# One change to an attention and two-expert-stage kernel: the second product's first operands are made a step earlier, its weights loaded tile by tile, and the start's hand-set order is written anew

## The chip, the cores and the metric

The kernel runs on one core of a Trainium2 chip. The metric is device time of one execution in microseconds (us); the lower the better. The engines named here are PE (TensorE, matrix products), DVE (VectorE, elementwise), ACT (ScalarE, activations and copies), POOL (GpSimd) and SP (SyncE, which issues nearly all DMAs). PEld is PE's weight load, which overlaps its matmuls.

## The reference, cut to what matters

```python
kv = np.einsum('bhsd,bhse->bhde', k, v)          # 4 batches, 8 heads, 576 rows, 64 columns
out = np.einsum('bhsd,bhde->bhse', q, kv)
x = out / np.sqrt(np.mean(out * out, axis=-1, keepdims=True) + 1e-06) * g_norm
x = x.transpose(0, 2, 1, 3).reshape(2304, 512)
x = ((x @ w_a) * (x @ w_b)) @ w_out              # w_a, w_b 512 x 1536, w_out 1536 x 512
h = x @ w_in                                     # w_in 512 x 2048
g = np.maximum(h, 0.0) + np.log1p(np.exp(-np.abs(h)))
return (g @ w2_out).astype(np.float32)           # w2_out 2048 x 512
```

All inputs are float32 or (the weights) 64-bit floats that the kernel itself narrows.

## The kernel before, in words

**Numbers in two halves.** Almost every matrix product is done three times, on a high and a low half of each operand (`P3`: high x high, high x low, low x high). Making the halves is called a split: ACT copies the value into the high half (L166, `half_hi`), then DVE subtracts that from the value and writes the low half (L169, `half_lo`). A split of a 128x512 tile is thus one ACT and one DVE instruction. In the traces `w` is a split weight, `x` a split attention output, `op` a split operand of the last two products, `ghl` a split gate.

**First part, the script.** Attention runs by batch (0 to 3) and head pair (0 to 3), the gated stage by slots: a slot is one block of 512 (or 256) rows with one of 12 chunks of 128 columns, and makes `a` and `b` (L951 in the first 12 slots, L922 after) out of weights `raw` that DMAs bring, DVE and ACT narrow (L190, L194, L199) and a split halves. The first 12 slots and all of the attention are written out by hand, word by word, in the string `SCRIPT`; with manual scheduling, PE, DVE, ACT and POOL run their instructions in that order. A word is a number (weight item, slot or batch), a letter and sometimes a further number: `W` load a weight (L182), `A`, `B`, `c` narrow it, `d` its high half, `e` its low half on DVE, `f` its low half on POOL; `k` and `K` load keys and values (L234, L235, L229, tile `kvraw`), `Q` queries (L288), `M` multiplies keys and values (L255), `O` queries by that product; `a0` to `b3` are the quarters of a slot. `H12` with no number ahead are 12 matmuls on constants (L964) that compute nothing and only keep PE at work.

**Middle.** The rest of the gated stage, slots 12 to 59, and its second product (L424).

**Last part, two pairs of row blocks.** The softplus stage does blocks 1 and 2 together (pair 0), then blocks 3 and 4 (pair 1), by a scheme that saves one product in eight: seven products in place of eight, each from sums and differences of the four quarters. For each pair, `stage1` is run for eight column pairs i; a step makes seven products (`x`, `y`, `z`, `v`, L591), adds them on DVE (L602) and takes softplus (`soft`: DVE L579, ACT L582, DVE L584), which gives four tiles `g` per step. `g_sums` (POOL, L654 and L655) makes the sums that the second product needs; it is called for step i - 1 in step i, and for the last step after it. In pair 1 a step also does the small block 0 (`single1`, `single2`: L792, L769, L775, tiles `h`, `gs`, `ghl`, `out`).

After the eight steps of a pair comes `stage2_2`: seven turns (`TURNS`: A11, S2, A12, S3, S1, A22, S4) of eight steps, 56 steps of 12 matmuls 128x256 (L750). A step needs one split operand `op` (ACT L166, DVE L169) and one half tile of weights `w2o`, loaded by DMA (L669). `operand` also issues one POOL subtraction for each operand of A11 (L690) and of A12 (L692), in place, after the split has read the tile. Operands are made three steps ahead (`AHEAD`). Weights are loaded a whole turn at a time, at the turn's first step for the next turn: four tiles, eight DMAs. `leave` takes a finished sum out of PSUM at a turn's end (L704 on DVE, L709 on ACT) and some of them are stored. In pair 0 this stage also carries, at the steps listed in `OPS_AT`, the 14 pieces of `op_steps(1)`, which make the split operands of pair 1's first stage out of `y` (L169 `op<-y`, L480, L481, L482, L499).

From slot 12 on, instructions of an engine go in the order that the scheduler gives them, which follows the program's order and its dependences. An engine works strictly in its order: an instruction that waits holds all behind it. SP's queue follows the program's order throughout.

Where `phase2` goes from one stage to the other, before:

```python
while flow:
    advance()
g_sums(i)
if pair:
    yield from single2(i)
yield from stage2_2(pair, [] if pair else list(zip(OPS_AT, op_steps(1))))
```

Of the kernel before, what the change touches and what calls it, by code (L numbers as in the profile page):

```python
# [73 lines left out]
0i 10W 1q1 1a1 0j 6f 1b1 1l1 2K 1M2 1a2 1q2 1b2 1l2 2K0 1a3 1M3 1g 2Q0 1q3 1b3 1V 2K1 1l3 2a0 1h 7B
2a1 1U 1i 2a2 2Q1 7A 8B 1O0 1j 2K2 1O1 7c 1S0 2a3 8A 9B 9A 1C0 2b0 2Q2 8c 2g 2b1 9c 1t0 2K3 10A 1O2
1S1 1u0 2b2 7d 1C1 2Q3 2b3 7f 1t1 1N0 2h 1S2 2Q 0s0 11W 1u1 1L0 1O3 2i 0s1 1E0 2j 0Q 1C2 0s2 1Q 1R0
3K 1N1 1t2 1X0 0s3 1L1 1u2 3a0 1S3 1Y0 1E1 3a1 3K0 1C3 1Z0 3a2 1R1 1N2 1H0 3Q0 1X1 3a3 1L2 1D0 2M0
1t3 3K1 1Y1 3g 2M1 1u3 1E2 1Z1 8d 3Q1 1N3 1R2 2M2 8e 3K2 1H1 1X2 3b0 1L3 1D1 9d 2M3 1Y2 1E3 3Q2 3b1
9e 2q0 3K3 3b2 1R3 1Z2 2q1 3b3 2l0 1H2 1X3 1s0 1q4 3Q3 3h 1s1 10B 1D2 3Q 3i 0O4 1Y3 2q2 1s2 0S4 3j
1s3 2q3 1Z3 0N4 0C4 2l1 4a0 1H3 1l4 0L4 4a1 1D3 11B 4a2 2l2 0E4 4a3 10c 3q0 0R4 2l3 4b0 4g 11A 4b1  # L80
0X4 10d 4b2 3q1 11c 1O4 2q4 10e 4b3 2V 0Y4 2s0 1S4 4h 2s1 11d 2U 4i 2s2 0Z4 1C4 2O0 4j 1t4 2O1 11e
0H4 2S0 2O2 1u4 2S1 0D4 2s3 2C0 3l0 5a0 2t0 3l1 5a1 2C1 2u0 2t1 5a2 2l4 2S2 2N0 3q3 2u1 5a3 2L0 3l3
5b0 5g 5b1 2E0 2C2 5b2 2t2 2N1 2R0 2u2 5b3 2L1 2X0 3s0 3q2 5h 1N4 2E1 3s1 2Y0 1L4 2N2 3l2 5i 3s2 2R1
# [1004 lines left out]
```

## Time and profile before

| | us |
|---|---|
| median of 3 runs | 882.71 (881.82 to 883.62) |
| the profiled execution, its own time | 884.52 |
| its span in the trace | 882.7 |
| busy in the span: PE | 861.1 (98%) |
| DVE | 607.0 (69%) |
| ACT | 399.4 (45%) |
| POOL | 116.8 (13%) |

The span is the stretch between the first and the last recorded instruction; the profiled execution took 1.8 us more than that. Busy time is the time in which an engine had an instruction in work. Of PE a share of 98% says that it hardly ever stood still, not that it ran at its peak: its matmuls overlap, and a matmul that runs at half clock is busy too.

### The profile page before, as it was taken

What the parts mean: (1) busy time and instruction counts of PE and PEld (TensorE: products, weight loads), DVE (VectorE), ACT (ScalarE), POOL (GpSimd) and SP (SyncE); (2) the same over time, 40 slices, a digit from 0 to 9 for tenths busy, and PEclk for the clock granted to TensorE, in tenths of its full rate; (3) what the DMA queues carried; (4) which work ended last, traced back from release to release, by engine and by line L of the source; (5) the groups of instructions that cost most, each with busy time, mean ns of one, the idle gap of its engine ahead of it and who ended that gap; (6) DMA issues with size and microseconds to landing.
All of it is one profiled execution on the core that took longest, in us unless ns stands there. A gap on an engine that the chain in (4) does not pass through costs nothing.

```text
span 882.7 us, 13219 instructions
## 1 busy us (share of the span) xinstructions
PE 861.1 (98%) x4974; PEld 745.0 (84%) x4974; DVE 607.0 (69%) x1003; ACT 399.4 (45%) x718; POOL 116.8 (13%) x80
## 2 busy tenths in 40 slices
...
GB/s 277 268 269 118 49 1 1 102 200 316 311 225 181 144 167 216 320 258 136 167 72 128 275 170 151 78 222 122 193 166 344 394 144 143 143 61 292 246 142 48
DMA packets 73070, 160.24 MB, mean 182 GB/s; under 512 B 6448, under 2 KB 41776, under 8 KB 73008
## 3 DMA queue, kind: packets, MB, share of 16 engines
...
q8 instruction: 39, 0.64, 0.3%
...
q10 hardware_dynamic: 144, 0.00, 0.0%
...
## 4 chain that ended last, share of the span: by engine, by line
PE 87%; DMA 6%; DVE 4%; SPq 1%; ACT 1%; issue 1%; DVEq 0%; ACTq 0%
PE acc L424 16%; PE acc L750 15%; PE b L922 12%; PE a L922 12%; PE x L591 5%; PE z L591 5%; PE v L591 5%; PE b L951 3%; PE a L951 3%; DMA kvraw<-in_kv 3%; PE y L591 2%; PE h L792 2%; PE acc L769 2%; DVE op L169 2%; PE o L314 1%; DMA w2o<-kept 1%
## 5 line engine op out<-in xcount | busy, mean ns | idle before, releaser
L750 PE MATMUL acc<-w2o,op 128*128 128x256 f32 x1344 | 166.2, 286 | 7.6 <-DVE op L169 4.3
L750 PEld LDWEIGHTS acc<-w2o,op 128*128 128x128 f32 x1344 | 163.9, 194 | 10.2 <-DVE op L169 6.4
L424 PE MATMUL acc<-ghl,w 128*128 128x512 f32 (+1 forms) x720 | 160.1, 369 | 0.0
L922 PE MATMUL b<-x,w 128*128 128x512 f32 (+1 forms) x576 | 146.6, 363 | 0.3 <-ACT w L166 0.3
L922 PE MATMUL a<-x,w 128*128 128x512 f32 (+1 forms) x576 | 146.6, 363 | 0.0
L424 PEld LDWEIGHTS acc<-ghl,w 128*128 128x128 f32 x720 | 125.7, 189 | 22.8 <-DVE y L454 0.2
L922 PEld LDWEIGHTS b<-x,w 128*128 128x128 f32 x576 | 101.7, 189 | 17.6 <-ACT w L166 0.7
L922 PEld LDWEIGHTS a<-x,w 128*128 128x128 f32 x576 | 102.0, 189 | 17.1
L393 DVE TENSOR_TENSOR g<-b,g 128x512 f32<-128x512 f32 (+1 forms) x60 | 38.2, 636 | 102.2 <-PE b L922 71.6
L654 POOL TENSOR_TENSOR s<-g 128x512 f32<-128x512 f32 x14 | 19.6, 1398 | 582.6 <-PE x L591 469.8
L389 ACT ACTIVATE g<-a 128x512 f32<-128x512 f32 (+1 forms) x60 | 33.2, 553 | 133.4 <-PE a L922 125.7
L169 DVE TENSOR_TENSOR op<-g,op 128x512 fp32r<-128x512 f32 x96 | 87.8, 978 | 0.1
L582 ACT ACTIVATE g<-g 128x512 f32<-128x512 f32 x64 | 39.6, 630 | 101.4 <-DVE g L579 101.2
L166 ACT ACTIVATE w<-raw 128x512 fp32r<-128x512 f32 x100 | 64.8, 670 | 17.0 <-DVE raw L199 12.3
L166 ACT ACTIVATE op<-g 128x512 fp32r<-128x512 f32 x96 | 54.0, 620 | 25.1 <-PE acc L750 16.9
L169 DVE TENSOR_TENSOR w<-raw,w 128x512 fp32r<-128x512 f32 x92 | 61.1, 686 | 3.3 <-ACT w L166 3.0
L194 ACT ACTIVATE raw<-raw 128x512 f32<-128x512 f32 x68 | 46.3, 683 | 26.7 <-DMA raw<-in_w_out 17.8
L169 DVE TENSOR_TENSOR ghl<-g,ghl 128x512 fp32r<-128x512 f32 (+1 forms) x60 | 39.2, 654 | 18.8 <-ACT ghl L166 18.7
L199 DVE SCALAR_TENSOR_TENSOR raw<-raw 128x512 int32<-128x512 int32 x68 | 49.0, 728 | 3.8 <-ACT raw L194 2.3
L166 ACT ACTIVATE ghl<-g 128x512 fp32r<-128x512 f32 (+1 forms) x60 | 35.2, 587 | 35.9 <-DVE g L393 33.6
L591 PE MATMUL v<-op,w 128*128 128x512 f32 x192 | 48.9, 389 | 0.0
L591 PE MATMUL z<-op,w 128*128 128x512 f32 x192 | 48.7, 389 | 0.0
...
## 6 DMA issues: line engine op xcount, KB each, us to landing
...
w2o<-kept SPq DMA_DIRECT2D x112, 256.0 KB, 5.0
...
```

What stands on the lines that cost most here:

```text
L166: nc.scalar.activation(out=hi, in_=src, func=AF.Copy)
L169: engine.tensor_tensor(out=lo, in0=src, in1=hi, op=ALU.subtract)
L194: nc.scalar.activation(out=high_f, in_=high_f, func=AF.Prelu, scale=HIGH_SCALE, alpha=SIGN_SCALE)
L199: nc.vector.scalar_tensor_tensor(out=low, in0=high, scalar=3, in1=low, op0=ALU.logical_shift_left, op1=ALU.bitwise_or)
L389: nc.scalar.activation(out=t, in_=a, func=AF.Copy)
L393: nc.vector.tensor_tensor(out=t, in0=b, in1=t, op=ALU.mult)
L424: nc.tensor.matmul(out=acc[j][i2][:, :n], lhsT=w[:, a, c2], rhs=g[:, c, :n], start=(opens and i == 0), stop=(closes and i == 2),)
L582: nc.scalar.activation(out=to, in_=to, func=AF.Softplus)
L591: nc.tensor.matmul(out=o, lhsT=w[:, a, (2 * k + kk) * P:(2 * k + kk + 1) * P], rhs=x[:, c, :], start=(start and kk == 0 and i == 0), stop= ...
L750: nc.tensor.matmul(out=set_[where][b][:, k * 256:(k + 1) * 256], lhsT=x[:, c, i2 * P:(i2 + 1) * P], rhs=w[:, a, :], start=(opens and cp == ...
L922: nc.tensor.matmul(out=o[:, :n], lhsT=w[:, a, kk * P:(kk + 1) * P], rhs=xhl[j, kk][:, c, :n], start=(kk == 0 and k == 0), stop=(kk == NK - ...
L951: nc.tensor.matmul(out=live[x, i], lhsT=wt[x, f][:, a, kk * P:(kk + 1) * P], rhs=xhl[j, kk][:, c, :], start=(kk == 0 and k == 0), stop=(kk ...
```

## The change

It has three parts.

**The script.** The order of the first 12 slots is written anew. All eight `f` (low half of a weight on POOL) become `e` (on DVE). Batch 0's keys and values of head pairs 1 to 3 come in one pair of DMAs in place of three. One of the 31 matmuls on constants goes. Weight 5 is loaded before batch 1's keys and values, and batch 1's head pair 3 of keys and values before the last query tile rather than after it. On PE batch 1's L255 products stand later among the slots' quarters.

**The second product.** A generator of `stage2_2` is made in the last step of `stage1` and run up to its new first `yield`: the first weight tile is loaded and the first three operands are made there, with their three L690. The rest follows where it stood. Weights are loaded one tile (two DMAs) at a time, a turn ahead.

**The pieces beside it.** `OPS_AT` moves most of the 14 pieces of `op_steps(1)` to later steps.

```diff
-OPS_AT = [4, 7, 10, 13, 18, 21, 26, 29, 34, 37, 48, 50, 52, 54]
+OPS_AT = [9, 13, 17, 21, 25, 29, 33, 36, 39, 42, 47, 49, 51, 53]
...
-H12 0k0 0K0 0Q0 0k1 0K1 0K2 0Q1 0k2 0Q2 0k3 0K3 0Q3 H4 0M0 0W 0v0 0O0 1W 0S0 0M1 2W 0N0 0v1 3W 0L0
+H12 0k0 0K0 0Q0 0k1 0K1 0Q1 0K2 0Q2 0K3 0Q3 H1 0M0 0W 0v0 0O0 1W 0S0 H2 0N0 2W 0M1 0L0 0E0 0V1 3W
...
-        def load(n):
+        def load(n, cp):
             if n < len(TURNS):
-                weights[n] = [t_load(TURNS[n][1], TURNS[n][2], (cp, cp + 1)) for cp in range(0, NCP, 2)]
+                weights[n, cp] = t_load(TURNS[n][1], TURNS[n][2], (cp, cp + 1))
...
-        load(0)
+        load(0, 0)
         for x in steps[:AHEAD]:
             operand(*x)
+        yield
+        for cp in range(2, NCP, 2):
+            load(0, cp)
...
-            if cp == 0:
-                load(n + 1)
-                if opens:
-                    set_[where] = [bank("acc") for _ in range(2)]
+            if cp == 0 and opens:
+                set_[where] = [bank("acc") for _ in range(2)]
...
-            if cp == NCP - 1:
-                weights.pop(n)
+            if cp % 2:
+                weights.pop((n, cp - 1))
+                load(n + 1, cp - 1)
...
+                    if k == 2 and i % NCP == NCP - 1:
+                        second = stage2_2(pair, [] if pair else list(zip(OPS_AT, op_steps(1))))
+                        next(second)
                     yield
...
-            yield from stage2_2(pair, [] if pair else list(zip(OPS_AT, op_steps(1))))
+            yield from second
...
-        "k": lambda b, p: kv_first(b, slice(p, p + 1)),
+        "k": lambda b, p: kv_first(b, slice(1, NK) if p else slice(0, 1)),
```

**What moves on PE in the script.** Of PE's order, the stretch in which batch 1's keys are multiplied by its values (`kvps`, two entries for each head pair); `a` and `b` are quarters of slots 1 and 2. Before, and then with the change, where head pairs 2 and 3 stand:

```order
L255 MATMUL kvps_344<-kvraw_214 64x64 x2
L255 MATMUL kvps_344<-kvraw_292 64x64 x8
L951 MATMUL a_386<-x_304,w_324 128x512 x3
L951 MATMUL b_395<-x_304,w_356 128x512 x3
L951 MATMUL a_386<-x_342,w_324 128x512 x3
L255 MATMUL kvps_344<-kvraw_214 64x64 x2
L255 MATMUL kvps_344<-kvraw_322 64x64 x8
L951 MATMUL b_395<-x_342,w_356 128x512 x3
```

```order
L255 MATMUL kvps_365<-kvraw_239 64x64 x2
L255 MATMUL kvps_365<-kvraw_301 64x64 x8
L957 MATMUL a_358<-x_331,w_337 128x512 x3
L957 MATMUL b_382<-x_331,w_348 128x512 x3
L957 MATMUL a_456<-x_208,w_363 128x512 x3
L255 MATMUL kvps_365<-kvraw_239 64x64 x2
L255 MATMUL kvps_365<-kvraw_329 64x64 x8
```

Before, head pair 3 (`kvraw_322`) stands ahead of the last quarter of slot 1's `b`; with the change (`kvraw_329`) that quarter and the first quarter of slot 2's `a` stand ahead of it.

**What moves on DVE and POOL at the end of pair 0's first stage.** First DVE; `p`, `c`, `z`, `v`, `x` belong to steps i = 6 (`_7`) and 7 (`_8`), `op_1` to `op_3` are the first three operands. Before:

```order
L602 TENSOR_TENSOR p_8_5210<-v_5207,p_8_5210 128x512
L584 SCALAR_TENSOR_TENSOR g_16_5209<-c_5262,g_16_5209 128x512
L579 TENSOR_SCALAR g_15_5208<-p_8_5210 128x512
L584 SCALAR_TENSOR_TENSOR g_15_5208<-p_8_5210,g_15_5208 128x512
L169 TENSOR_TENSOR op_1_5292<-g_1_4631,op_1_5292 128x512
L169 TENSOR_TENSOR op_2_5296<-g_3_4744,op_2_5296 128x512
L169 TENSOR_TENSOR op_3_5300<-g_5_4824,op_3_5300 128x512
```

With the change:

```order
L579 TENSOR_SCALAR g_13_5131<-x_5127 128x512
L584 SCALAR_TENSOR_TENSOR g_14_5132<-c_5158,g_14_5132 128x512
L169 TENSOR_TENSOR op_1_5235<-g_1_4626,op_1_5235 128x512
L584 SCALAR_TENSOR_TENSOR g_13_5131<-x_5127,g_13_5131 128x512
L602 TENSOR_TENSOR c_5185<-z_5129,p_7_5133 128x512
L169 TENSOR_TENSOR op_2_5239<-g_3_4739,op_2_5239 128x512
L579 TENSOR_SCALAR g_14_5132<-c_5185 128x512
L602 TENSOR_TENSOR p_7_5133<-v_5130,p_7_5133 128x512
L169 TENSOR_TENSOR op_3_5243<-g_5_4819,op_3_5243 128x512
L584 SCALAR_TENSOR_TENSOR g_14_5132<-c_5185,g_14_5132 128x512
L579 TENSOR_SCALAR g_13_5131<-p_7_5133 128x512
L602 TENSOR_TENSOR p_8_5205<-y_5200,p_8_5205 128x512
```

Before, the splits stand behind the last L584 of the first stage; with the change three of them stand among the additions and softplus pieces of step 6, ahead of all of step 7's (`p_8`). On POOL in the same place, `s_7` and `s_8` being sums of steps 6 and 7; the rows of the difference, before and then with the change:

```order
L655 TENSOR_TENSOR g_12_5065<-g_11_5064,g_12_5065 128x512
L654 TENSOR_TENSOR s_7_5226<-g_14_5137 128x512
L655 TENSOR_TENSOR g_14_5137<-g_13_5136,g_14_5137 128x512
L654 TENSOR_TENSOR s_8_5277<-g_16_5209 128x512
L655 TENSOR_TENSOR g_16_5209<-g_15_5208,g_16_5209 128x512
L690 TENSOR_TENSOR g_1_4631<-s_1_4762,g_1_4631 128x512
L690 TENSOR_TENSOR g_3_4744<-s_2_4842,g_3_4744 128x512
```

```order
L655 TENSOR_TENSOR g_12_5060<-g_11_5059,g_12_5060 128x512
L690 TENSOR_TENSOR g_1_4626<-s_1_4757,g_1_4626 128x512
L690 TENSOR_TENSOR g_3_4739<-s_2_4837,g_3_4739 128x512
L690 TENSOR_TENSOR g_5_4819<-s_3_4917,g_5_4819 128x512
L654 TENSOR_TENSOR s_7_5221<-g_14_5132 128x512
L655 TENSOR_TENSOR g_14_5132<-g_13_5131,g_14_5132 128x512
L654 TENSOR_TENSOR s_8_5287<-g_16_5204 128x512
L655 TENSOR_TENSOR g_16_5204<-g_15_5203,g_16_5204 128x512
```

Three L690 now stand ahead of the sums of steps 6 and 7; the other five follow them. In pair 1 the same move puts the three splits behind `ghl` of step 14, among the first L602 of step 15.

**What moves on DVE ahead of the 22nd operand.** Pair 0's `stage2_2`; `op_5628` and its like are splits of `y`. Before:

```order
L169 TENSOR_TENSOR op_18_5572<-g_3_4744,op_18_5572 128x512
L169 TENSOR_TENSOR op_19_5588<-g_5_4824,op_19_5588 128x512
L704 TENSOR_TENSOR s_1_5598<-acc_5465,c_1_5440 128x512
L704 TENSOR_TENSOR s_2_5606<-acc_5466,c_2_5448 128x512
L169 TENSOR_TENSOR op_20_5620<-g_7_4904,op_20_5620 128x512
L169 TENSOR_TENSOR op_21_5636<-g_9_4984,op_21_5636 128x512
L169 TENSOR_TENSOR op_22_5652<-g_11_5064,op_22_5652 128x512
L169 TENSOR_TENSOR op_5668<-y_1977,op_5668 128x512
```

With the change:

```order
L169 TENSOR_TENSOR op_21_5605<-g_9_4979,op_21_5605 128x512
L704 TENSOR_TENSOR s_1_5576<-acc_5442,c_1_5429 128x512
L704 TENSOR_TENSOR s_2_5584<-acc_5443,c_2_5437 128x512
L480 TENSOR_TENSOR s_5624<-y_1972,y_1976 128x512
L480 TENSOR_TENSOR s_5700<-y_1974,y_1978 128x512
L481 TENSOR_TENSOR y_1972<-y_1704,y_1972 128x512
L481 TENSOR_TENSOR y_1974<-y_1706,y_1974 128x512
L482 TENSOR_TENSOR y_1704<-s_5624,y_1704 128x512
L482 TENSOR_TENSOR y_1706<-s_5700,y_1706 128x512
L169 TENSOR_TENSOR op_5628<-y_1704,op_5628 128x512
L169 TENSOR_TENSOR op_22_5631<-g_11_5059,op_22_5631 128x512
```

Before, the six L480 to L482 stood between operands 11 and 15; with the change all six stand behind the two L704, directly ahead of operand 22. Up to operand 26 four splits of `y` stand there in place of six.

## Rows read from the trace of the kernel before

**Rows 1.** Windows: us; busy us (count) of PE, PEld, DVE, ACT, POOL; clock; DMA; GB/s.

```profile
20.00:46.00 26.00, 21.41 (x163) 15.65 (x163) 22.62 (x32) 18.36 (x33) 11.54 (x7) 1.00 1.05 286
46.00:212.00 166.00, 166.00 (x940) 139.27 (x940) 107.28 (x195) 111.65 (x215) 1.32 (x1) 1.00 0.38 118
212.00:400.00 188.00, 187.72 (x906) 158.28 (x906) 136.11 (x259) 90.79 (x158) 0.00 (x0) 1.00 0.62 232
400.00:577.00 177.00, 177.00 (x850) 149.35 (x849) 114.79 (x198) 56.75 (x99) 20.12 (x14) 1.00 0.43 151
628.00:673.00 45.00, 44.98 (x374) 44.83 (x374) 29.22 (x49) 18.96 (x34) 0.00 (x0) 1.00 0.61 207
```

**Rows 2.** Waits of PE: in total, times, longest.

```profile
PE acc L750 <- DVE op L169: 4.3, 4, 1.4
```

**Rows 3.** Timeline of PE, 20 to 46 us: start, length, work, idle ahead of it.

```profile
43.71 0.69 PE L255 MATMUL kvps<-kvraw 112*64 112x64 f32 x16 [1.28 <-DMA kvraw<-in_kv]
```

**Rows 4.** DMA issues, 16 to 46 us: KB each, median us to landing.

```profile
qr<-in_q SPq DMA_DIRECT2D x5, 256.0 KB, 12.0
```

**Rows 5.** The weight tiles w on POOL: ns lowest, median, highest; idle before.

```profile
L169 POOL TENSOR_TENSOR w<-raw,w x8: 1307/1613/2035, 21.9 to 52.0; 128x512 fp32r<-128x512 f32 x8
...
  ACT w L166: 25.7, 5
```

**Rows 6.** The same tiles on DVE, first 220 us.

```profile
L169 DVE TENSOR_TENSOR w<-raw,w x22: 680/684/693, 62.7 to 216.7; 128x512 fp32r<-128x512 f32 x22
...
  ACT w L166: 1.9, 3
```

**Rows 7.** Timeline of PE around the end of pair 0's first stage.

```profile
581.12 1.52 PE L591 MATMUL v<-op,w 128*128 128x512 f32 x6
585.90 0.80 PE L750 MATMUL acc<-w2o,op 128*128 128x256 f32 x2 [3.26 <-ACT op L166]
...
602.26 20.41 PE L750 MATMUL acc<-w2o,op 128*128 128x256 f32 x168 [0.90 <-DVE op L169]
```

**Rows 8.** Windows, columns as in the first group.

```profile
590.00:592.00 2.00, 2.00 (x12) 2.00 (x12) 2.00 (x3) 1.04 (x3) 2.00 (x2) 0.54 0.02 1
```

**Rows 9.** Timeline of DVE in the same part.

```profile
575.85 1.00 DVE L584 SCALAR_TENSOR_TENSOR g<-p,g 128x512 f32<-128x512 f32 x1 [0.70 <-ACT g L582]
...
578.60 0.69 DVE L602 TENSOR_TENSOR c<-v,c 128x512 f32<-128x512 f32 x1 [0.35 <-PE v L591]
...
584.25 0.42 DVE L579 TENSOR_SCALAR g<-p 128x512 int32<-128x512 int32 x1
...
586.26 12.54 DVE L169 TENSOR_TENSOR op<-g,op 128x512 fp32r<-128x512 f32 x8
...
605.74 1.88 DVE L169 TENSOR_TENSOR op<-g,op 128x512 fp32r<-128x512 f32 x3
...
614.80 1.28 DVE L704 TENSOR_TENSOR s<-acc,c 128x512 f32<-128x512 f32 x2
...
627.39 3.09 DVE L169 TENSOR_TENSOR op<-g,op 128x512 fp32r<-128x512 f32 x5
```

**Rows 10.** Timeline of POOL in the same part.

```profile
588.10 13.56 POOL L690 TENSOR_TENSOR g<-s,g 128x512 f32<-128x512 f32 x8 [0.63 <-DVE op L169]
...
614.42 8.50 POOL L692 TENSOR_TENSOR g<-g 128x512 f32<-128x512 f32 x5 [0.70 <-DVE op L169]
```

**Rows 11.** Timeline of PE around the end of pair 1's first stage.

```profile
795.27 0.40 PE L750 MATMUL acc<-w2o,op 128*128 128x256 f32 x2
796.82 16.37 PE L750 MATMUL acc<-w2o,op 128*128 128x256 f32 x123 [1.15 <-DVE op L169]
```

**Rows 12.** Timeline of DVE ahead of it.

```profile
779.02 0.69 DVE L602 TENSOR_TENSOR p<-y,p 128x512 f32<-128x512 f32 x1 [1.06 <-PE y L591]
780.31 0.69 DVE L602 TENSOR_TENSOR c<-z,p 128x512 f32<-128x512 f32 x1 [0.60 <-PE z L591]
781.67 0.69 DVE L602 TENSOR_TENSOR c<-v,c 128x512 f32<-128x512 f32 x1 [0.67 <-PE v L591]
```

More of the change, by code (lines that the diff above doesn't have):

```diff
@@ L74 @@
[L74 to L83, printed above, removed]
@@ new lines @@
+0O1 0R0 0X0 0M2 0S1 4W 0Y0 0N1 0v2 0Z0 0O2 0L1 5W 0H0 0M3 0S2 0D0 0E1 6W 0V3 0N2 0R1 0A 0B 0O3 0X1
+0L2 1K 0c 0E2 0Y1 0S3 1A 0R2 H3 0N3 0Z1 1K0 1B 0X2 0H1 1c 0L3 0D1 0d 1Q0 0E3 0Y2 1K1 1d 0e 0R3 0Z2
+H9 0a0 2B 0X3 1Q1 0H2 1e 3B 1K2 0D2 4B H3 0b0 0Y3 5B 0a1 2A 0b1 0Z3 1Q2 6B 0a2 2c 1K3 0H3 3A 0b2 2d
+4A 0D3 3c 1Q3 0a3 2e 3d 0b3 7W 4c 0g 1a0 3e 4d 1M0 0h 8W 1q0 1b0 5A 0i 1l0 1a1 0j 9W 1b1 5c 1M1 1q1
+4e 5d 6A 1a2 10W 1l1 1b2 5e 1M2 6c 2K 1q2 1a3 6d 1l2 1b3 1g 6e 2a0 2K0 1h 1M3 1q3 2a1 1i 1l3 1V 2Q0
@@ new lines @@
+2a2 1j 7B 2a3 2K1 7A 1U 2b0 2g 7c 2b1 8B 8A 2Q1 1O0 7d 8c 2K2 1O1 1S0 7e 8d 2b2 9A 1C0 2b3 8e 1t0
+2Q2 1O2 2h 1S1 2K3 0s0 9B 1u0 2i 10A 1O3 9c 1C1 0s1 1t1 2j 2Q3 1N0 1S2 1u1 2Q 0s2 1L0 11W 0s3 1C2
+1E0 3a0 1t2 0Q 3a1 1R0 1u2 1Q 3a2 1S3 3K 1X0 9d 3a3 1Y0 1C3 1N1 3g 9e 3b0 3K0 1L1 1Z0 1N2 1t3 3b1
+1H0 1u3 3b2 1E1 3Q0 1D0 1L2 3b3 3K1 1R1 1s0 3h 1E2 1s1 1X1 2q0 1N3 1R2 1Y1 3Q1 2M0 3i 2l0 3K2 1L3
+1s2 1Z1 10B 2M1 1X2 1E3 3j 1H1 1s3 3Q2 1Y2 1R3 2M2 3K3 1q4 1D1 2q1 0O4 1Z2 2q2 1X3 2M3 1H2 3Q3 1l4
+0S4 4a0 1Y3 3Q 2q3 4a1 1D2 0C4 11B 1Z3 4a2 2l1 1H3 1O4 10c 3q0 1D3 10d 2l2 2V 4a3 10e 1S4 4b0 2U 4g
@@ new lines @@
+4b1 1C4 2l3 2O0 1t4 11A 2O1 2q4 3l0 2S0 1u4 4b2 2S1 11c 4b3 2C0 2l4 2s0 2t0 4h 2C1 1N4 2s1 2u0 2t1
+2O2 4i 2u1 1L4 2N0 4j 2S2 2s2 2L0 2s3 1E4 5a0 2E0 5a1 1R4 2R0 5a2 1X4 2C2 2X0 5a3 2t2 1Y4 0N4 11d
+2O3 2Y0 5g 2u2 0L4 5b0 2S3 2Z0 5b1 0E4 1Z4 5b2 2H0 11e 5b3 1H4 2D0 0R4 3s0 5h 2C3 3s1 1D4 2t3 2N2 5i
+0X4 2N1 2L2 2u3 3M0 2L1 5j 2E2 3s2 0Y4 2E1 3s3 0Z4 2R2 6a0 2R1 2X2 3x0 6a1 2X1 3x1 6a2 2Y2 3x2 2N3
+2Y1 3x3 6a3 2Z2 0H4 6b0 2L3 2Z1 6g 6b1 0D4 2H1 6b2 2H2 2D1 6b3 2E3 2D2 4s0 3q1 6h 2R3 4s1 3l1 3q2
@@ new lines @@
+2O4 2X3 6i 3q3 3l2 4s2 6j 2S4 3M1 2Y3 2C4 3l3 2t4 4s3 2Z3 3M2 2u4 2H3 7a0 2D3 3M3 2N4 3V 7a1 2L4 7a2
+3U 3q4 7a3 2E4 3l4 3O0 7g 2R4 7b0 3S0 7b1 2X4 3C0 7b2 2Y4 3t0 3O1 2Z4 3O2 3u0 3S1 2H4 7b3 3C1 5s0
+2D4 3t1 7h 3N0 3S2 5s1 3u1 7i 3O3 3L0 7j 3C2 5s2 3E0 3N1 3t2 5s3 3R0 3u2 8a0 3L1 3X0 8a1 3S3 3Y0 3E1
+8a2 3C3 3Z0 8a3 3R1 3N2 8g 3X1 8b0 3H0 3Y1 8b1 3L2 3D0 3t3 8b2 3E2 3Z1 8b3 3u3 3R2 6s0 8h 3H1 3N3
+3X2 8i 6s1 3D1 3L3 6s2 8j 3E3 6s3 3Y2 3R3 9a0 3Z2 9a1 3X3 3H2 9a2 3Y3 9a3 3D2 9b0 9g 3Z3 3O4 3H3 3D3
```

20 lines of the change are left out of this document (5 added, 15 removed).

## Prediction

> **What bounds the kernel now.** I read the windows first: from 46 to 577 us PE is busy for all but 0.3 us, and from 628 to 673 us for all but 0.02 of 45 us [rows 1]. There nothing but fewer matmuls would help, and the change leaves the same matmuls and, from slot 12 to step 6 of pair 0's first stage, the same order on every engine. What can be won lies where PE stands still: 26.00 - 21.41 = 4.6 us between 20 and 46 us [rows 1] and the changes from a first to a second product. The list of PE's waits puts 4.3 us on DVE's operand splits alone [rows 2], so I went on to the timelines of PE, DVE and POOL at those two places.
>
> The yardstick is the second product's pace: 44.98 us for 374 matmuls [rows 1] are 0.1203 us each, 1.443 us for a step of 12.
>
> **The script.** PE waits 1.28 us for batch 1's last keys and values; it is at them at 43.71 - 1.28 = 42.43 us [rows 3]. The change takes one query tile of 256 KB [rows 4] out from ahead of them; at the 286 GB/s of that window [rows 1] these are 0.9 us, so they land near 42.8. It also puts two quarters, six matmuls, ahead of that product. If they only fill the wait, the 1.28 us are gone. I take **1.3 us**. Bounds: no more than the 4.6 us that PE stands still there; on the other side a loss, since eight low halves go from POOL to DVE (below, the third rival). On POOL they took 1.61 us each [rows 5], on DVE such a half takes 0.68 [rows 6]. The dropped matmul on constants and the merged loads of batch 0 cost or save nothing that a row shows, since DMA is full through that window at a share of 1.05 and moves the same bytes [rows 1].
>
> **Pair 0's turnover.** PE ends the first stage at 581.12 + 1.52 = 582.64 us and then waits 3.26 us for the first operand [rows 7]. At full pace step 25 could begin at 582.64 + 25 x 1.443 = 618.7. It begins when operand 26 is done, at 627.39 + 0.68 = 628.07 [rows 9]: 9.4 us are lost, though the first wait was 3.3. The rest is DVE, which has no gap from 586.26 on. Alone it issues a split every (1.88 - 0.68) / 2 = 0.60 us [rows 9]. Beside POOL's L690, 1.70 us each (13.56 / 8), it makes one per POOL instruction [rows 9, 10]; I price a POOL instruction beside it at 1.70 - 0.60 = 1.10 us of DVE. This fits: from operand 1 to operand 26 there are 40 DVE instructions and 16 POOL ones, 40 x 0.60 + 16 x 1.10 = 41.6 us, and the trace has 628.07 - 586.26 = 41.8.
>
> With the change the first three operands are ready, and PE runs three steps, to 582.64 + 4.33 = 586.97. But the three splits and three L690 are not gone, they stand on DVE ahead of the last step's softplus: 3 x 0.60 + 3 x 1.10 = 5.1 us. DVE's idle time there hides 0.70 + 0.35 = 1.05 of it [rows 9]; L579 on `p`, at 584.25 before, comes 4.05 us later, at 588.3, and operand 4 begins at 588.7. From there to operand 26 there are 36 DVE instructions (two splits of `y` less) and 13 POOL ones, 36 x 0.60 + 13 x 1.10 = 35.9, so 624.6. PE gets operand 4 at 588.7 + 1.7 = 590.4, after a stand of 3.4 us.
>
> Now the clock. Before, PE's wait of 3.26 us is followed by a granted clock of one half (1.2 GHz), and of 0.54 over 590 to 592 [rows 8], so full again at about 591.8: 5.9 us after its first matmul at 585.90. A stand of 3.4 us is as long, so I reckon with the same 5.9 us at half after it. PE then makes 2.05 steps by 596.3 and comes to step 25 after another 19.95 x 1.443 = 28.8 us, at 625.1; without the half clock DVE's 624.6 holds. I take the later, 625.1: **3.0 us**. The Trainium skill (TensorE: Matmul & The Clock Gate, Part 1) has the rule that the gate follows how busy PE has recently been and halves the clock of an idle one. By that rule too the sum is 3.0, and where the stand is short enough to leave the clock alone it is 3.5; the trace agrees as far as its 0.54 goes.
>
> How many DVE instructions the three moved L690 stretch is what I know least. The two L704, which read PSUM, ran 0.64 us each while POOL was busy [rows 9, 10], and several L602 and L584 on that stretch read PSUM too. With one L690 beside such work, all times fall by 1.1 and the gain is 4.1. The Trainium skill (SBUF — State Buffer, Who interferes with whom) has the rule: a DVE instruction with two SBUF inputs is shut out by a POOL instruction that reads SBUF, one with at most one is not. The L704 row agrees; by the rule the gain would be 4.1, by a price for every L690 it is 3.0. I stay with 3.0, as L584 on `c` and `p` has both inputs in SBUF. Ends: 9.4, if DVE were never late; 0, if DVE gets no time back and only the order of its work changes.
>
> **The block ahead of operand 22.** Six L480 to L482 stand now directly ahead of operand 22, and L692 follow operand 17, so five of these may run beside them. Operand 22 is the 31st instruction from operand 4: 588.7 + 31 x 0.60 + 10 x 1.10 = 618.3, and PE, with the half clock, is ready for it at 596.3 + 15.95 x 1.443 = 619.3. I cost the block at nothing for that reason; it is 1 us away from being a wait.
>
> **Pair 1's turnover.** From 795.27 to 796.82 + 16.37 = 813.19 there are 125 matmuls [rows 11], 15.04 us at the yardstick: 2.88 us lost, on operands 3 to 8 beside eight L690. With three operands made ahead and five L690 left, PE has 4.33 us of work while DVE makes the next ones at 1.70 each, behind operand 4; steps take 1.443, so the start lasts for the five. The splits stand where DVE idles for 1.06 + 0.60 + 0.67 = 2.33 us [rows 12], among L602 that read PSUM: 3 x 0.60 + 1.10 (operand 3 beside the first L690) - 2.33 = 0.6 us later `ghl`, for which PE already waits. 2.88 - 0.6 = **2.3 us**. Ends: 2.9 with no delay; 0.1 if all three L690 stretch DVE (3 x 1.70 - 2.33 = 2.8).
>
> **Weights tile by tile.** The loads go out in the same order on SP, a turn ahead of their use, 8 x 1.443 = 11.5 us. I cost them at nothing: the matmuls run ahead of them at full pace in 628 to 673 us [rows 1], where no wait for a load stands. If that cover were gone, PE would wait at each turn.
>
> **Sum.** 1.3 + 3.0 + 2.3 = 6.6 us off the profiled execution's 884.52 us (span 882.7 and 1.8 around it): 877.9. The median shown is 1.81 below that execution, so I predict **876.1 us** for the median.
>
> **The rivals.**
> *More than the sum.* DVE is not late at pair 0: 9.4 there, 1.3 and 2.3 elsewhere, 13.0 us: 869.7. For it speak the L704; against it that DVE's work is only moved, and that it has 1.05 us of idle time to put it in.
> *Only moved.* PE's stand after step 2 or ahead of operand 22 gives back all that pair 0 wins (another 3.0 us, half of 5.9 us at half clock, if the stand comes behind step 20). Then 1.3 + 2.3 = 3.6 are left: 879.1.
> *No change.* `kvraw` lands as late as before, because DMA is full; pair 0 gives 0 and pair 1 0.1: 882.6. For it: DVE is without gaps in both. Against it: 2.33 us of idle time at pair 1 is there to be used.
> *Slower.* On POOL the eight low halves waited 25.7 us for their high halves [rows 5] and held nobody else. On DVE such a wait holds all behind it, the attention's additions and gates that PE needs. DVE's own such waits took 1.9 / 3 = 0.63 us [rows 6]; eight waits and eight halves are 8 x (0.63 + 0.60) = 9.8 us. If PE stands still for all of it, and the turnovers give their 5.3, it is 4.5 us slower: 887.2. It decides from a loss of 5.3 + 1.8 = 7.1 us on in the script. Against it: DVE's splits and narrowing in that window are freed of POOL, which was busy for 11.54 of 26 us [rows 1].
>
> **How the numbers follow.** 0.2% of 882.71 is 1.8 us, about what a measurement of this kernel can tell from no change. The forecast, with a gain of 4 to 10 us, gets 0.50; more than 10 us 0.09; only moved (1.8 to 4 us) 0.20; no change 0.11; slower 0.10. So faster 0.79, same 0.11, slower 0.10. The range runs from 871.0 to 881.5: that is the forecast, "only moved" and the gains between the forecast and the first rival, and it leaves out most of "more than the sum", "no change" and "slower", of whose 0.30 some third lies inside.
>
> **What would show it.** Right: PE's first L750 follows the last L591 with no wait; a stand of 2 to 4 us comes behind its third step, waiting for DVE's fourth split; step 25 begins near 625; in pair 1 L750 runs without a wait for DVE; the 1.28 us wait for `kvraw` is gone and the middle part, from slot 12 to pair 0's first stage, starts about 1.3 us earlier and lasts as long as before. Wrong: a wait of PE for an attention or weight half between 46 and 80 us, a wait for `w2o`, or step 21 waiting for operand 22 with the clock at a half after it.

## The result, and the profile after

| | before | with the change |
|---|---|---|
| median, us | 883.02 (881.82 to 883.62, 4 runs) | 875.78 (874.70 to 876.59, 4 runs) |
| profiled execution: span, us | 882.7 | 874.4 |

The ratio is 0.9918, 95% interval 0.9907 to 0.9930: 0.8% faster, 7.2 us. Forecast were 876.1 us and a gain of 6.6.

The page's line of busy times of the changed kernel: POOL has lost the eight low halves, and DVE, which has them now, is busy for 604.3 us in place of 607.0.

```profile
PE 859.2 (98%) x4972; PEld 743.6 (85%) x4972; DVE 604.3 (69%) x1013; ACT 399.0 (46%) x716; POOL 108.0 (12%) x72
```

To place the gain I read three marks off PE's timeline in each trace: the first product `x` of the softplus stage (what lies ahead is attention and gated stage), the first `x` of pair 1, and the end of the last matmul of the second product.

| us | start to first `x` | pair 0 | pair 1 |
|---|---|---|---|
| before | 505.9 | 166.9 | 206.1 |
| with the change | 503.9 | 162.9 | 203.9 |
| difference | -2.0 | -4.0 | -2.2 |
| predicted | -1.3 | -3.0 | -2.3 |

The differences of these two executions add to 8.2 us, 1.0 more than the medians differ; the one of the kernel before took 884.52 us, 1.5 over its median, and its start was late (experiments, below).

The list of PE's waits after (in total, times, longest). Operand splits on DVE cost 2.6 us in place of 4.3 [rows 2], and the 3.3 us for the first operand [rows 7] are gone; new are the 0.8 for `c` and, double its 0.8 of before, the wait for `ghl`:

```profile
PE acc L751 <- DVE op L169: 2.6, 4, 1.7
...
PE acc L771 <- ACT ghl L166: 1.6, 1, 1.6
PE ms L332 <- ACT sq L321: 1.4, 3, 1.0
PE z L591 <- DVE c L602: 0.8, 1, 0.8
...
PE a L957 <- DVE x L169: 0.6, 1, 0.6
```

PE around the end of pair 0's first stage, the counterpart of [rows 7]. There is now no gap ahead of the first L751; there is one of 0.78 ahead of `z` in the last step. The stand behind the third step is 0.16 us, and a second one of 1.67 comes two steps on. At step 21 PE waits for operand 22, first 0.45 us for ACT's high half and, a matmul later, 0.43 for DVE's low half. After the 301 matmuls ahead of the row at 622.12, PE is at step 25. Counted from the last step's `x` (578.40 before), that is 45.7 us against 628.07 - 578.40 = 49.7.

```profile
576.41 1.52 PE L591 MATMUL x<-op,w 128*128 128x512 f32 x6
578.71 1.66 PE L591 MATMUL z<-op,w 128*128 128x512 f32 x6 [0.78 <-DVE c L602]
...
581.57 4.59 PE L751 MATMUL acc<-w2o,op 128*128 128x256 f32 x37
586.32 3.39 PE L751 MATMUL acc<-w2o,op 128*128 128x256 f32 x24 [0.16 <-DVE op L169]
591.38 23.17 PE L751 MATMUL acc<-w2o,op 128*128 128x256 f32 x191 [1.67 <-DVE op L169]
615.00 0.38 PE L751 MATMUL acc<-w2o,op 128*128 128x256 f32 x1 [0.45 <-ACT op L166]
615.80 6.01 PE L751 MATMUL acc<-w2o,op 128*128 128x256 f32 x48 [0.43 <-DVE op L169]
622.12 8.06 PE L751 MATMUL acc<-w2o,op 128*128 128x256 f32 x65 [0.31 <-DVE op L169]
```

DVE in the same stretch, the counterpart of [rows 9], and the three L690 moved ahead, to be read beside it as [rows 10]:

```profile
570.87 0.68 DVE L602 TENSOR_TENSOR c<-z,p 128x512 f32<-128x512 f32 x1
571.46 0.81 DVE L169 TENSOR_TENSOR op<-g,op 128x512 fp32r<-128x512 f32 x1
...
572.54 0.68 DVE L602 TENSOR_TENSOR p<-v,p 128x512 f32<-128x512 f32 x1
573.14 1.18 DVE L169 TENSOR_TENSOR op<-g,op 128x512 fp32r<-128x512 f32 x1
...
574.85 1.51 DVE L579 TENSOR_SCALAR g<-p 128x512 int32<-128x512 int32 x1
...
584.14 0.42 DVE L579 TENSOR_SCALAR g<-p 128x512 int32<-128x512 int32 x1
584.48 3.48 DVE L169 TENSOR_TENSOR op<-g,op 128x512 fp32r<-128x512 f32 x2
...
606.67 1.41 DVE L704 TENSOR_TENSOR s<-acc,c 128x512 f32<-128x512 f32 x2 [1.81 <-PE acc L751]
...
621.39 2.48 DVE L169 TENSOR_TENSOR op<-g,op 128x512 fp32r<-128x512 f32 x4
```

```profile
570.43 1.31 POOL L690 TENSOR_TENSOR g<-s,g 128x512 f32<-128x512 f32 x1 [3.92 <-DVE op L169]
572.36 1.41 POOL L690 TENSOR_TENSOR g<-s,g 128x512 f32<-128x512 f32 x1 [0.62 <-DVE op L169]
574.40 1.68 POOL L690 TENSOR_TENSOR g<-s,g 128x512 f32<-128x512 f32 x1 [0.62 <-DVE op L169]
```

The three L690 do not cost the same. Under the first one L602 (570.87) reads PSUM and takes its 0.68 us; operand 2's split takes 0.81, operand 3's under the second 1.18, both in place of 0.68, and the L579 on `p` under the third 1.51 in place of 0.42: 1.7 us in all where I had 3 x 1.10 = 3.3. L579 on `p` comes 7.7 us after the last step's `x`, against 584.25 - 578.40 = 5.9 before: 1.9 us later, not 4.05. At 606.67 DVE even waits 1.81 us for PE, with the block of L480 to L482 still ahead of it.

PE at pair 1's turnover, the counterpart of [rows 11]. The wait for `ghl` stands at 1.59 us, and the second product runs without a gap. The first row is the same wait in the kernel before:

```profile
792.15 3.29 PE L769 MATMUL acc<-w,ghl 128*128 128x512 f32 x12 [0.82 <-ACT ghl L166]
```

```profile
786.96 0.73 PE L771 MATMUL acc<-w,ghl 128*128 128x512 f32 x2 [1.59 <-ACT ghl L166]
...
790.18 25.00 PE L751 MATMUL acc<-w2o,op 128*128 128x256 f32 x207
```

### The profile page after: what moved, and what is told of

It reads as the page before. It is cut to its first block, busy times and chain, and to the rows that moved or that the text cites. A ratio compares the mean times of both kernels' runs of the same rounds, so it can differ in the third digit from the quotient of the medians.

```text
span 874.4 us, 13195 instructions
## 1 busy us (share of the span) xinstructions
PE 859.2 (98%) x4972; PEld 743.6 (85%) x4972; DVE 604.3 (69%) x1013; ACT 399.0 (46%) x716; POOL 108.0 (12%) x72
## 4 chain that ended last, share of the span: by engine, by line
PE 91%; DVE 5%; ACT 2%; issue 1%; DMA 1%; DVEq 0%; ACTq 0%
PE acc L424 17%; PE acc L751 16%; PE b L928 12%; PE a L928 12%; PE x L591 5%; PE v L591 5%; PE z L591 5%; PE a L957 4%; PE b L957 4%; PE y L591 2%; PE h L794 2%; PE acc L771 2%; PE o L314 1%; PE kvps L255 1%; DVE op L169 1%
## 5 line engine op out<-in xcount | busy, mean ns | idle before, releaser
L751 PE MATMUL acc<-w2o,op 128*128 128x256 f32 x1344 | 163.3, 283 | 3.0 <-DVE op L169 2.6
L751 PEld LDWEIGHTS acc<-w2o,op 128*128 128x128 f32 x1344 | 162.0, 192 | 4.5 <-DVE op L169 3.6
L654 POOL TENSOR_TENSOR s<-g 128x512 f32<-128x512 f32 x14 | 19.7, 1407 | 617.3 <-DVE g L584 617.3
L169 DVE TENSOR_TENSOR op<-g,op 128x512 fp32r<-128x512 f32 x96 | 81.0, 894 | 3.0 <-ACT op L166 2.7
L169 DVE TENSOR_TENSOR w<-raw,w 128x512 fp32r<-128x512 f32 x100 | 66.5, 685 | 3.7 <-ACT w L166 3.2
L169 DVE TENSOR_TENSOR ghl<-g,ghl 128x512 fp32r<-128x512 f32 (+1 forms) x60 | 38.1, 635 | 18.5 <-ACT ghl L166 18.4
L591 PE MATMUL z<-op,w 128*128 128x512 f32 x192 | 48.9, 390 | 0.8 <-DVE c L602 0.8
L199 DVE SCALAR_TENSOR_TENSOR raw<-raw 128x512 int32<-128x512 int32 x68 | 46.4, 688 | 3.8 <-ACT raw L194 2.6
L591 PE MATMUL v<-op,w 128*128 128x512 f32 x192 | 48.9, 389 | 0.0
```

The source lines that it names most:

```text
L169: engine.tensor_tensor(out=lo, in0=src, in1=hi, op=ALU.subtract)
L199: nc.vector.scalar_tensor_tensor(out=low, in0=high, scalar=3, in1=low, op0=ALU.logical_shift_left, op1=ALU.bitwise_or)
L591: nc.tensor.matmul(out=o, lhsT=w[:, a, (2 * k + kk) * P:(2 * k + kk + 1) * P], rhs=x[:, c, :], start=(start and kk == 0 and i == 0), stop= ...
L751: nc.tensor.matmul(out=set_[where][b][:, k * 256:(k + 1) * 256], lhsT=x[:, c, i2 * P:(i2 + 1) * P], rhs=w[:, a, :], start=(opens and cp == ...
```

## The experiments

Times are medians beside runs of the kernel before on the same chip; the ratio is to those. "In us" is the ratio's distance from 1 times 882.7.

| kernel | us | ratio, 95% | in us | first `x` | pair 0 | pair 1 |
|---|---|---|---|---|---|---|
| script only | 882.29 | 0.9994 (0.9985 to 1.0002) | -0.5 | 502.1 | 166.9 | 206.1 |
| list of steps only | 882.39 | 0.9995 (0.9986 to 1.0003) | -0.4 | 504.5 | 166.1 | 206.1 |
| tile loads only | 878.40 | 0.9949 (0.9937 to 0.9961) | -4.5 | 503.7 | 165.2 | 203.3 |
| early call and tile loads | 878.45 | 0.9951 (0.9939 to 0.9963) | -4.3 | 505.4 | 164.0 | 203.9 |
| operands before loads | 881.08 | 0.9977 (0.9966 to 0.9987) | -2.0 | 504.5 | 163.6 | 205.9 |
| early call only | 880.50 | 0.9976 (0.9964 to 0.9988) | -2.1 | 503.2 | 164.1 | 207.3 |
| change, old script | 876.66 | 0.9929 (0.9911 to 0.9947) | -6.3 | 503.6 | 162.9 | 203.9 |
| change, no early call | 876.19 | 0.9933 (0.9920 to 0.9945) | -5.9 | 503.1 | 164.1 | 203.3 |
| change, `kvraw` behind query | 875.00 | 0.9921 (0.9908 to 0.9933) | -7.0 | 501.9 | 162.9 | 203.9 |
| change, low halves on POOL | 876.24 | 0.9935 (0.9922 to 0.9949) | -5.7 | 503.5 | 162.9 | 203.9 |
| change, L690 and L692 on DVE | 872.43 | 0.9878 (0.9859 to 0.9897) | -10.8 | 503.6 | 160.7 | 202.9 |
| the same, last sums on DVE | 871.47 | 0.9879 (0.9865 to 0.9892) | -10.7 | 503.1 | 159.6 | 203.3 |

The start to the first `x` varies from one execution to the next, with the old script by 2.6 us over seven traces (503.2 to 505.9). The two other columns repeat to 0.1 us where the code is the same, and are the better evidence.

**The parts alone: the script.** The whole new text of the script with the one line for `k`:

```diff
-"k": lambda b, p: kv_first(b, slice(p, p + 1)),
+"k": lambda b, p: kv_first(b, slice(1, NK) if p else slice(0, 1)),
```

> The kernel before with the new script alone (and the merged loads of batch 0 that belong to it). My theory: the new order takes PE's waits at the start away and nothing else; the first product of the softplus stage comes 2.0 us earlier, as in the changed kernel, and all behind it lasts as long as before, so the time is 881.0 us, 2.0 below before. Rival: the turnover of pair 0 is where the 2.0 us are kept, because DVE is free earlier there; then the script alone gives under 1 us. In the trace PE's 1.28 us wait for kvraw is gone in either case.

It is 0.5 us faster, and its interval takes in no change. Pair 0 and pair 1 last as before, so nothing is kept there. The rival falls, and so does the 2.0.

**The early call with the tile loads**, old list and old script:

```diff
+            for cp in range(2, NCP, 2):
+                load(0, cp)
...
+                    if k == 2 and i % NCP == NCP - 1:
+                        second = stage2_2(pair, [] if pair else list(zip(OPS_AT, op_steps(1))))
+                        next(second)
```

> The kernel before with the first three operands made in the last step of the first stage and the weights loaded tile by tile, the old list of steps for the pieces beside it and the old script. My theory: the early operands alone carry the gain of both turnovers, 4.0 us at pair 0 and 2.2 at pair 1, less the two splits of y that the old list puts ahead of operand 26 (2 x 0.60 us): 883.0 - 5.0 = 878.0 us. Rival: the new list does half of pair 0's gain, and then early operands alone give only about 2 us there and 2.2 at pair 1: 878.8 to 879, with a wait for DVE of more than 3 us ahead of step 12.

4.3 us: 2.9 at pair 0 and 2.2 at pair 1. The time lies between the two expectations and decides nothing alone; by pairs the trace is near the theory's 4.0 - 1.2 = 2.8 and 2.2, not the rival's 2 and 2.2. PE's waits for DVE ahead of step 12 are 0.17, 1.67 and 1.12 us, together just under the rival's 3.

**The list of steps:**

```diff
-OPS_AT = [4, 7, 10, 13, 18, 21, 26, 29, 34, 37, 48, 50, 52, 54]
+OPS_AT = [9, 13, 17, 21, 25, 29, 33, 36, 39, 42, 47, 49, 51, 53]
```

> The kernel before with the new list of steps for the pieces beside pair 0's second product, nothing else. My theory: two splits of y fewer ahead of operand 26, 1.2 us of DVE at 0.60 each, and no more, 881.8 us, as the first wait and the eight L690 stay. Rival: the list does half of pair 0's gain by itself, 2 us, 881.0. If the six L480 to L482 ahead of operand 22 cost a new wait, it is 883 or more.

Pair 0 is 0.75 us shorter in the trace; by the times it is 0.4 us, which can't be told from nothing. On top of the early call the list gives pair 0 a further 164.0 - 162.9 = 1.1 us.

**The tile loads**, with everything else as before:

```diff
-        def load(n):
+        def load(n, cp):
...
-        load(0)
+        load(0, 0)
         for x in steps[:AHEAD]:
             operand(*x)
+        for cp in range(2, NCP, 2):
+            load(0, cp)
...
+            if cp % 2:
+                weights.pop((n, cp - 1))
+                load(n + 1, cp - 1)
```

> The kernel before with its second product's weights loaded one tile at a time, nothing else. My theory: nothing, 883.0 us within 0.5, since no wait for a weight stands in the second product before or after. Rival: the loads' place matters at the turnover, where SP's queue holds stores; then pair 1's start moves by 1 us or more either way.

This was my mistake: 4.5 us, as much as with the early call. PE of this kernel around pair 0's turnover has no first wait either:

```profile
580.25 3.15 PE L750 MATMUL acc<-w2o,op 128*128 128x256 f32 x25
...
587.36 3.40 PE L750 MATMUL acc<-w2o,op 128*128 128x256 f32 x24 [2.02 <-DVE op L169]
592.43 4.58 PE L750 MATMUL acc<-w2o,op 128*128 128x256 f32 x36 [1.67 <-DVE op L169]
```

DVE's order of this kernel shows how. Nothing in the program puts the splits into the last step, and yet they stand there, the first 2.8 us behind the last `x` (578.94 - 576.17), where with the change it runs 6.8 ahead of it (569.66, 576.41):

```
L584 SCALAR_TENSOR_TENSOR g_16_5209<-c_5235,g_16_5209 128x512
L169 TENSOR_TENSOR op_1_5283<-g_1_4631,op_1_5283 128x512
L584 SCALAR_TENSOR_TENSOR g_15_5208<-x_5204,g_15_5208 128x512
L602 TENSOR_TENSOR c_5262<-z_5206,p_8_5210 128x512
L169 TENSOR_TENSOR op_2_5287<-g_3_4744,op_2_5287 128x512
```

The operand is the tile 5283 here, the next one taken after the first weight tile; before it was 5292, behind four weight tiles. All of them come from one pool of 38 buffers. So I held that the place in the pool, and not the transfer, is what counts. The two kernels as they are built fit this: before, the buffer of the first operand was last read by the last step's `x` product (L591), here by the `x` of the step before it.

**The same with the loads left whole:**

```diff
-        load(0)
         for x in steps[:AHEAD]:
             operand(*x)
+        load(0)
```

> The kernel before with two lines exchanged: the first three operands of the second product are taken before its first four weight tiles, and loads still come a whole turn at a time. Operands and weight tiles take their buffers from one pool of 38 in program order. My theory after the first runs: the gain of the tile-by-tile loads is that the operands stand for earlier buffers, which come free a step earlier, so that the scheduler can put their splits among the last step's softplus; then this exchange gives most of what the tile loads alone gave, 4.3 us at most, 878.4 to 879.5 us. Rival: the loads themselves matter (when SP issues them); then the exchange gives nothing, 882.7 us.

2.0 us, between theory and rival, but at each pair the trace is clear. Pair 0 is 3.3 us shorter, without any change to how loads are cut. Pair 1 gains only 0.1: its splits are early as well, but now the weights are late. PE of this kernel there, and then SP's queue and its longest wait from 770 to 800 us:

```profile
790.62 4.47 PE L750 MATMUL acc<-w2o,op 128*128 128x256 f32 x36
797.50 17.74 PE L750 MATMUL acc<-w2o,op 128*128 128x256 f32 x146 [2.41 <-DMA w2o<-kept]
```

```profile
772.93 1.84 SPq L669 DMA_DIRECT2D w2o<-kept  x3
791.70 2.47 SPq L780 DMA_DIRECT2D out<-out  x4
```

```profile
SPq L780 <- DVE out L775: 16.9, 1, 16.9
```

All loads but three stand behind the stores of `out` (L780), which wait 16.9 us for DVE's last additions; in the kernel before it is all but five. The program writes these stores ahead of every load of the second product, so SP's queue does not keep the program's order here, though I had said that it does throughout. So both matter: operands early in the pool, the first weight tile before them. Taking one weight tile, three operands and then the other tiles is what serves both. The exchange moves the operands in the pool and in the program's order at once; which of the two lets the scheduler place the splits earlier is not shown.

**The early call alone**, behind four weight tiles:

```diff
         load(0)
         for x in steps[:AHEAD]:
             operand(*x)
+        yield
...
+                        next(second)
```

> The kernel before with the early call alone: the generator of the second product is run up to the first three operands in the last step, behind a load of all four weight tiles of the first turn; later turns load whole turns, old list, old script. Theory of the prediction: the early call is what makes the operands ready, PE begins without a wait, and it gives 4 to 5 us, 878 to 878.7 us. Rival by the buffers: four weight tiles and then the next turn's four still stand ahead of the operands, which then wait for buffers, and it gives under 2 us: 881 to 882.7 us.

Only 2.1 us. Pair 0 gains 2.8, but pair 1 loses 1.2: there the three splits run in one piece, 2.98 us, ahead of the last step's softplus, and `ghl` is so late that PE stands for 3.49 us. DVE's row, then PE's:

```profile
776.89 2.98 DVE L169 TENSOR_TENSOR op<-g,op 128x512 fp32r<-128x512 f32 x3
```

```profile
789.43 0.72 PE L770 MATMUL acc<-w,ghl 128*128 128x512 f32 x2 [3.49 <-ACT ghl L166]
```

**The change without the early call:**

```diff
-                    if k == 2 and i % NCP == NCP - 1:
-                        second = stage2_2(pair, [] if pair else list(zip(OPS_AT, op_steps(1))))
-                        next(second)
```

> The changed kernel without the early call: the second product is begun after the first stage as before, with the new script, the new list and the tile-by-tile loads. After the runs so far I hold that the tile loads let the scheduler put the three splits into the last step anyway, only some 8 us later in it; the early call then adds what the traces of early and tiles alone differ by, 1.2 us won at pair 0 and 0.5 lost at pair 1: 876.5 us, 0.7 above the changed kernel. Rival, the prediction's own view: the call is what makes the operands ready, and without it the turnovers lose 4 us or more: 880 us.

5.9 us of the change's 7.2 remain, so the call adds 1.3 by the ratios, whose intervals meet, and 0.7 by the traces: 1.26 won at pair 0, 0.54 lost at pair 1, where PE waits for `ghl` only the 0.82 us of the kernel before. PE in this kernel starts the second product without a wait too; it stands longer behind its third step.

```profile
579.75 3.15 PE L750 MATMUL acc<-w2o,op 128*128 128x256 f32 x25
...
586.86 3.39 PE L750 MATMUL acc<-w2o,op 128*128 128x256 f32 x24 [2.02 <-DVE op L169]
```

**The script on top of the rest:**

> The changed kernel with the old script. If the script is worth the 1.3 us of the prediction, 877.1 us; if it is worth what the two traces show for the start (2.0 us), 877.8; if it is worth the 0.4 us that it gave alone, 876.2. In the trace the start of the softplus stage's first product tells it, but this has lain between 503.7 and 505.9 us in four traces with the old script, so the times decide.

The edit takes `SCRIPT` and the line for `k` back. 6.3 us remain, so the script gives 0.9 us here and gave 0.5 alone. The waits that it removes are not the one that I had named. PE's waits at the start of this kernel, with the old script:

```profile
PE b L957 <- ACT g L389: 1.4, 1, 1.4
...
PE a L957 <- POOL w L169: 0.8, 1, 0.8
...
PE b L957 <- POOL w L169: 0.7, 1, 0.7
```

There is no wait for `kvraw` in it, nor in the five other traces with the old script but that of the kernel before. That one execution had its transfers late at the start (PE was busy for 37.0 of the first 46 us, in the other six for 39.0 to 39.3). In the six traces with the new script and its low halves on DVE it is 40.4 to 40.5, 1.1 to 1.5 us more than in those six; so in PE's work at the start the script shows more than in the times, whose intervals don't exclude 1.3.

**Where the `kvraw` of head pair 3 stands on SP:**

```diff
-1K3 0H3 3A 0b2 2d
+1Q3 0H3 3A 0b2 2d
...
-4A 0D3 3c 1Q3 0a3
+4A 0D3 3c 1K3 0a3
```

> The changed kernel with the last query tile again ahead of batch 1's last keys and values on SP. By the prediction those then land 0.9 us later and PE, which is at them at about 41.8 us in the changed kernel, waits for kvraw up to about 1 us: 876.5 us. Rival: by the two quarters that now stand ahead, PE comes to them late enough in any case, and no wait for kvraw appears: 875.8 us.

No wait appears, and the time is that of the change. The 256 KB that I built the script's term on are worth nothing. (The word `1K3` stands ahead of `1Q3` in the old script too; on SP's queue of all seven traces with it the query tile goes first; in the kernel before the last two query tiles are issued from 28.81 us on, the keys and values at 30.82. It is this order that the edit brings back.)

**Low halves back on POOL** (the eight `e` that were `f` before become `f` again):

> The changed kernel with the eight low halves of the first weights back on POOL. The prediction's slower rival took the move to DVE for a cost of up to 9.8 us in waits of DVE; if there is such a cost, this kernel is faster than the changed one by a us or more. My theory: the move is about even, DVE wins back at 1.10 us for each what it spends at 0.60, and PE's wait for POOL's w returns for the first slots: 876 to 877 us.

The ratio is 0.9935 against the change's 0.9918: 1.5 us slower, with intervals that meet, and not faster. The windows of the first 46 us, of the changed kernel, of the change with the old script and of this one, agree: PE gets 40.46, 38.96 and 39.80 us of work done there, so 0.7 of the script's 1.5 is the move of the low halves.

```profile
0.00:46.00 46.00, 40.46 (x302) 29.60 (x303) 30.45 (x61) 29.38 (x53) 1.60 (x8) 1.00 0.99 307
```

```profile
0.00:46.00 46.00, 38.96 (x300) 28.00 (x301) 30.14 (x51) 29.07 (x54) 12.79 (x15) 1.00 0.99 313
```

```profile
0.00:46.00 46.00, 39.80 (x302) 28.91 (x303) 29.75 (x54) 28.96 (x52) 12.37 (x15) 1.00 0.99 304
```

**The price of POOL beside DVE.** L690 and L692 on DVE:

```diff
-                nc.gpsimd.tensor_tensor(out=a11, in0=s1g[i], in1=a11, op=ALU.subtract)
+                nc.vector.tensor_tensor(out=a11, in0=s1g[i], in1=a11, op=ALU.subtract)
...
-                nc.gpsimd.tensor_tensor(out=a12, in0=a12, in1=a11, op=ALU.subtract)
+                nc.vector.tensor_tensor(out=a12, in0=a12, in1=a11, op=ALU.subtract)
```

> The changed kernel with the subtractions of L690 and L692 on DVE in place of POOL. My price of a POOL instruction beside DVE is 1.10 us of DVE, a DVE instruction takes 0.60 at its pace; by this DVE gains 0.5 us for each of the subtractions that ran beside it, PE's waits for DVE in pair 0 (2.6 us, and 0.8 in the last step) shrink, and the kernel takes about 2 us less than the changed one, 873.8 us. Rival: the price is wrong since not every POOL instruction stretches DVE; then DVE has 32 more instructions of 0.60 us, and where it is late it is later: 876 to 878 us.

10.8 us faster than before, 3.5 more than the change, where I expected 2. DVE has 32 instructions more and is busy for 5 us less, as its line of the page shows, and the subtraction itself takes 0.68 us in place of 1.69 (the second row is that of the changed kernel):

```profile
PE 857.6 (98%) x4972; PEld 742.9 (85%) x4972; DVE 599.1 (69%) x1045; ACT 399.0 (46%) x716; POOL 49.2 (6%) x40
```

```profile
L690 DVE TENSOR_TENSOR g<-s,g x16: 676/683/1184, 571.2 to 793.7; 128x512 f32<-128x512 f32 x16
```

```profile
L690 POOL TENSOR_TENSOR g<-s,g x16: 1289/1692/1747, 570.4 to 798.5; 128x512 f32<-128x512 f32 x16
```

PE in this kernel around pair 0's turnover. From 590.93 on it has no gap; the stand of 1.67 us is down to 0.71, and the one behind the third step has grown to 0.83; the one for `c` in the last step stays at 0.83:

```profile
581.40 4.59 PE L751 MATMUL acc<-w2o,op 128*128 128x256 f32 x37
586.82 3.40 PE L751 MATMUL acc<-w2o,op 128*128 128x256 f32 x24 [0.83 <-DVE op L169]
590.93 41.30 PE L751 MATMUL acc<-w2o,op 128*128 128x256 f32 x342 [0.71 <-DVE op L169]
```

What is left there is DVE with the last two POOL instructions, L654 and L655, beside it: two splits in 3.49 us, 1.1 us each above their pace.

```profile
584.98 3.49 DVE L169 TENSOR_TENSOR op<-g,op 128x512 fp32r<-128x512 f32 x2
```

**The last sums on DVE too:**

```diff
+        e = nc.vector if i % NCP == NCP - 1 else nc.gpsimd
-        nc.gpsimd.tensor_tensor(out=t, in0=a21, in1=a22, op=ALU.add)
-        nc.gpsimd.tensor_tensor(out=a21, in0=a11, in1=a21, op=ALU.subtract)
+        e.tensor_tensor(out=t, in0=a21, in1=a22, op=ALU.add)
+        e.tensor_tensor(out=a21, in0=a11, in1=a21, op=ALU.subtract)
```

> The kernel with L690 and L692 on DVE, which took 872.43 us, with the last step's two sums (L654, L655) on DVE too. In that kernel two splits took 3.49 us beside these two POOL instructions, 1.1 each more than alone; two more DVE instructions cost 1.2. By the price PE's waits of 0.83 and 0.71 us ahead of steps 3 and 5 of pair 0 shrink by about 1 us together, and pair 1 is as before: 871.4 us. Rival: the splits wait for something else there, the sums only make DVE later: 872.4 us or more.

In the trace the two waits shrink from 0.83 and 0.71 to 0.23 and 0.36, and pair 0 is 1.15 us shorter, as priced; pair 1 is 0.4 longer, its wait for `ghl` 1.10 us in place of 0.68. The times don't show it: the ratio is that of the kernel without this edit, 0.9879 to 0.9878.

```profile
585.73 2.04 PE L752 MATMUL acc<-w2o,op 128*128 128x256 f32 x14 [0.23 <-DVE op L169]
588.14 44.06 PE L752 MATMUL acc<-w2o,op 128*128 128x256 f32 x365 [0.36 <-DVE op L169]
```

## Why the prediction was right, and where it was not

The sum was 6.6 us, 7.2 were measured. That they lie so close is in part luck: pair 0 gave 1.0 more than its term, and the script, by the times, 0.4 to 0.8 less. The terms one by one:

**The script (1.3).** The cause was wrong, the size is open: 0.5 to 0.9 by the times, 1.1 to 1.5 by PE's work in the first 46 us. I took a wait of 1.28 us for `kvraw` for a property of the kernel. It belonged to that one execution: six other traces of the same script have none, and moving the transfer changes nothing. The gain comes from waits for ACT's gate (1.4) and for POOL's low halves (1.5), which go, while others come or grow (DVE's `x` 0.6 and `w` 0.5, ACT's `sq` 1.4 in place of 0.9). The slower rival, with DVE held by eight more halves, is refuted: POOL with them back is not faster.

**Pair 0 (3.0).** 4.0 in the trace. PE does begin at once, and DVE is later in the last step, as said. It was mis-sized: I priced all three moved L690 at 1.10, 3.3 us, and 1.7 were paid, so operand 4 begins 584.48 - 576.41 = 8.1 us after the last step's `x`, where I had 588.7 - 578.40 = 10.3, and the stand that I expected to be 3.4 us was 0.16 and 1.67. With that the half clock, 5.9 us of it, did not come: the granted clock is 1.00 in every window from 570 to 626 us. Against this, operands 4 to 26 took DVE 37.6 us in place of 35.9 (operand 26 is the first of the four splits at 621.39): it waited 1.81 us for PE, and the 13 POOL instructions that I counted leave out the last step's L654 and L655, beside which operands 4 and 5 took 3.48 us. The lower price, one L690 beside instructions that read PSUM, gave 4.1 and was the better one.

**The block ahead of operand 22 (nothing).** Here a wait came that the sum puts at nothing, 0.45 and 0.43 us at step 21. I had PE there 619.3 - 578.40 = 40.9 us after the last step's `x`, and the operand 1 us sooner; with shorter stands and no half clock PE's last matmul of step 20 ends at 591.38 + 23.17 - 576.41 = 38.1, ahead of it. The clock stayed at 1.00 behind this wait.

**Pair 1 (2.3).** 2.2. `ghl` is late by 1.59 - 0.82 = 0.8 us where I had 0.6, and the gaps of the second product are gone.

**Weights tile by tile (nothing).** Here a step failed. I costed the tiles at nothing because no wait for a weight stands in the second product, and gave the whole gain to the early call. Alone, the tiles give 4.5 us and the call 2.1; on top of all else the call gives 1.3. By pairs: at pair 0 the call alone gives 2.8 us, the tiles alone 1.6, and both 2.9, so there the call would have been enough; at pair 1 the call alone loses 1.2, the tiles alone give 2.8, and both 2.2, so there the gain is that of the tiles. The rows of the order that I counted with were those of both together, so the sum did not suffer; the explanation did. That the order of taking tiles moves the splits is shown by one exchange of lines for pair 0, and only argued for the rest; why the scheduler then places them earlier stays open.

**The list (two splits fewer, 1.2 us of DVE).** 0.75 to 1.1 us in the traces, in line.

**The rivals.** "More than the sum" and "only moved" both had a grain: DVE's work was only moved, but a part of it went to places where POOL costs it nothing.
